# An adaLN attention and gMLP block on one core: the projection stage rearranged (transposes rounded by ScalarE from PSUM, four V tiles in step, w_qkv in column halves, modulation sums spread)

## The chip, the cores and the metric

The kernel runs on one core of one Trainium2 chip. A core has five engines that run side by side, each through its own queue in order: TensorE (PE, matrix multiplication; PEld is its weight load), VectorE (DVE), ScalarE (ACT), GpSimd (POOL) and SyncE (SP), which here only issues DMAs. They meet through semaphores. Data lie in SBUF (128 partitions), matmuls write into PSUM banks, and only PE, DVE and ACT are used on PSUM here. The metric is the device time of one execution in microseconds (us), the median of the runs.

## The reference

A block with S = 2048 tokens, D = 448 channels and 16 heads of 28 channels, in float32:

```
mod = (silu(c) @ w_mod).reshape(1, 6, 1, -1)
sa, ca, ga, sb, cb, gb = (mod[:, i] for i in range(6))
h = layernorm(x) * (1 + ca) + sa
q, k, v = split(h @ wqkv)                       # 16 heads of 28
x = x + ga * (softmax(q k^T / sqrt(28)) v @ wo)
h = layernorm(x) * (1 + cb) + sb
z = gelu(h @ w_in);  z1, z2 = halves(z);  z2 = layernorm(z2)
out = x + gb * ((z1 * (w_sp @ z2 + b_sp)) @ w_out)
```

The change touches the way to q, k and v: the modulation `mod`, the first layer norm, its transposition and the projection `h @ wqkv`.

## The kernel before

**Precision.** PE multiplies a rounded format (`F32R`). To keep float32 accuracy a matrix is stored as a rounded high part `hi` and the rest `lo` (`sub`, L69 to 71: the full value minus `hi`), and a product is made from hi·hi, hi·lo and lo·hi. D = 448 is 3 chunks of 128 and a last one of 64; the last chunk is put on partitions 0 to 63 and again on 64 to 127, so that one matmul handles two parts of it. `STEPS` lists the 11 resulting matmuls. So a V tile (128 tokens, 448 channels) and a QK unit (128 of the 896 rows of q and k, 512 tokens) are 11 matmuls each.

**The order is written by hand.** The program runs under a manual schedule: each engine executes its instructions in the order in which the Python text issues them. PSUM banks come from a ring of seven (`ring`) and one more bank (`ps_o`) that the attention stage uses for its outputs. SBUF buffers rotate within a pool by name or tag, and a DMA into one is issued only when the previous use of that buffer is over; as SP's queue is in order, a DMA behind it waits too.

**Stages.** Tokens are handled in four groups `g` of 512 (four tiles of 128). In order:

- Loads (L149 to 176): `x` of group 0, four slices `wm` of `w_mod` (one pair of the three pairs of modulation vectors), then the V columns of `wqkv` in four chunks. The q and k columns are read by `load_w("qk", i)`, 896 columns at a time, after group 0's transposes.
- Modulation: `mod_acc(pair, k)` (L194 to 201) is one of four steps of VectorE that add up a pair's vectors over slices of `w_mod` in `acc`. `mod_col` (L203 to 211) turns a vector into per-partition columns (`col_ca`, `col_sa`, and later `col_sb`, `col_cb`) with five one-column matmuls for each vector and an add by VectorE; `mod_bc` (L213 to 216) broadcasts one over all partitions. Pair 0 is needed at once; pairs 1 and 2 are needed only after the attention stage has begun (`ga` and the second layer norm).
- Layer norm: `ln_stats(g)` (L220 to 234) takes mean and variance on VectorE and the reciprocal root `rs` on GpSimd (L94, L95). `ln_norm(g)` (L235 on) writes `xn` on VectorE (L238) and has GpSimd copy its last 64 columns once more (L248).
- `ln_transpose` (L97 to 124): 16 transposes on PE (L104) fill four banks `tp`; each chunk is scaled and shifted from PSUM into `hfull` (ACT L111 or DVE L113), rounded to `hi` (L118 or L120), and `lo` is subtracted (L71). In group 0 ScalarE takes chunks 0 and 1 and VectorE chunks 2 and 3; in the other groups ScalarE takes all four, and GpSimd subtracts. In group 0 the columns are made between the transposes and these steps, and PE runs small matmuls on constants (`pe_fill`, L190) beside them.
- `v_tiles` (L251 to 258) and `qk_unit` (L260 to 273). A QK unit is copied out by ScalarE (`qf`), rounded by ScalarE (`qh`), its low part subtracted by GpSimd (`ql`), and both are stored to DRAM (`qk_scr`) by SP.
- The loop over `g` (L316 to 374). For each group: two V tiles, transposes of group g+1, statistics and normalisation of group g+2, two more V tiles, then QK units m = 0 and 3. Group 0 makes three V tiles ahead (two of them in step), then the hi and lo parts of the q and k weights (`weight_part`, L77 on, ScalarE for hi, VectorE and GpSimd in turn for lo), and a memset of V's spare columns (L362). Group 3 makes its QK units before its V tiles and begins to load head 0. `mod_acc` of pairs 1 and 2 stand at the end of groups 1 and 2; `mod_bc("ga")` and `mod_col(sb)` stand in group 2, the last pair's after the loop.
- A stretch of 20 QK units (m = 4, 1, 5, 2, 6 for four groups) in which each unit carries four score matmuls `mt` (`m_first`, `m_mm`, L385 to 393): scores of head 0 and part of head 1 for the row maximum, which VectorE reduces (L393). 80 `mt` in all.
- Then the attention loop over heads, the output projection and the gMLP, which the change leaves alone.

Of the kernel before, what the change touches and what calls it, by code (L numbers as in the profile page):

```python
# [20 lines left out]
NG = 4  # L21
# [12 lines left out]
def tile_adaln_mha_gmlp(ctx, tc, x, wqkv, wo, w_in, w_spT, b_sp, w_out, cT, w_mod, out):  # L34
# [35 lines left out]
    def sub(eng, dst, a, hi):  # L70
        eng.tensor_tensor(out=dst, in0=a, in1=hi.bitcast(F32), op=ALU.subtract)  # L71
# [2 lines left out]
        eng.dma_start(dst[0:64], src)  # L74
        eng.dma_start(dst[64:128], src)

    def weight_part(dst, i, raw, hi_eng, lo_eng, zero=True):  # L77

        n = raw.shape[-1]
        h = dst[:, i if i < 3 else 6, :n]  # L80
        if hi_eng is act:
            act.activation(h, raw, AF.Copy)
        else:
            hi_eng.tensor_copy(h, raw)
        if i < 3:
            sub(lo_eng, dst[:, 3 + i, :n], raw, h)
        else:
            sub(lo_eng, dst[0:64, 7, :n], raw[0:64], h[0:64])
            if zero:
                pool.memset(dst[64:128, 7, :n].bitcast(F32), 0.0)  # L90

    def rstd_of(var, rs, n):

# [54 lines left out]

    def load_mod(pair, eng):  # L149
        for k in range(4):  # L150
            wms[pair, k] = e1.tile([112, 2, D], F32, name="wm", bufs=4)
            eng.dma_start(wms[pair, k], w_mod[:, pair, k])

    def load_x(g, eng):
# [3 lines left out]
        for t in range(4):  # L158
            xts[4 * g + t] = xg[:, t, :]

    def load_w(kind, i, eng):
        c0, n = (2 * D, D) if kind == "v" else (0, 2 * D)
        raw = e1.tile([128, 2 * D], F32, name="raw", bufs=4)[:, :n]
        if i < 3:
            eng.dma_start(raw, wqkv[i * 128 : (i + 1) * 128, c0 : c0 + n])
        else:
            load_z(eng, raw, wqkv[384:448, c0 : c0 + n])
        raws[kind, i] = raw

    cc_t = e1.tile([112, 4], F32, name="cc_t", bufs=1)  # L170
    sp.dma_start(cc_t, cT)
# [1 line left out]
    load_mod(0, sp)  # L173
    for i in (0, 2, 1, 3):
        load_w("v", i, sp)
    pool.memset(wv[64:128, 7, :].bitcast(F32), 0.0)
    pool.memset(wqk[64:128, 7, :].bitcast(F32), 0.0)

# [6 lines left out]

    wu = ring.tile([128, 512], F32, name="wu", tag="s")

    def pe_fill(n):
        for _ in range(n):
            pe.matmul(wu[:, 0:128], ones, ones, start=True, stop=True)  # L190

    accs = {}

# [6 lines left out]
        else:  # L200
            dve.scalar_tensor_tensor(out=acc, in0=wm, scalar=silu[:, k : k + 1], in1=acc, op0=ALU.mult, op1=ALU.add)

    def mod_col(*parts):  # L203
        pc = ring.tile([128, 512], F32, name="pc", tag="s")
        for i, (nm, acc, plus1) in enumerate(parts):
            for c, r, e in ((0, 0, 128), (1, 0, 128), (2, 0, 128), (3, 0, 64), (3, 64, 128)):
                pe.matmul(
                    pc[r:e, 4 * i + c : 4 * i + c + 1], acc[:, c * 128 : c * 128 + e - r], ones[:112, 0:1], start=True, stop=True
                )
        for i, (nm, acc, plus1) in enumerate(parts):  # L210
            dve.tensor_scalar(out=cols[nm], in0=pc[:, 4 * i : 4 * i + 4], scalar1=plus1, scalar2=None, op0=ALU.add)

    def mod_bc(nm, acc):  # L213
        pc = ring.tile([128, 512], F32, name="pc", tag="s")
# [18 lines left out]
    def ln_norm(g):  # L233
        mv, rs = mv1.pop(g)
        res = []  # L235
        for t in range(4):
            xn = e1.tile([128, 512], F32, name="xn", bufs=4)
            dve.tensor_scalar(  # L238
                out=xn[:, :D],
                in0=xts.pop(4 * g + t),  # L240
                scalar1=mv[:, t, 0:1],
                scalar2=rs[:, t : t + 1],
                op0=ALU.subtract,
                op1=ALU.mult,
            )
            res.append(xn)
        for xn in res:
            pool.tensor_copy(xn[:, D:], xn[:, 384:D])  # L248
        return res

    def v_tiles(*kts):  # L251
        pvs = [ring.tile([128, 512], F32, name="pv", tag="s") for _ in kts]
        for j, (a, b) in enumerate(STEPS):
            for kt, pv in zip(kts, pvs):
                g, t = divmod(kt, 4)
                pe.matmul(pv[:, :D], hT[g][:, a, t * 128 : (t + 1) * 128], wv[:, b, :], start=j == 0, stop=j == NST - 1)  # L256
        for kt, pv in zip(kts, pvs):
            dve.tensor_copy(V[:, kt, :, 0:DH], pv[:, :D].rearrange("p (h d) -> p h d", d=DH))

    def qk_unit(m, g, mid=None):  # L260
        pq = ring.tile([128, 512], F32, name="pq", tag="s")
        for j, (a, b) in enumerate(STEPS):
            if mid and j in mid:
                mid[j]()
            pe.matmul(pq, wqk[:, b, m * 128 : (m + 1) * 128], hT[g][:, a, :], start=j == 0, stop=j == NST - 1)  # L265
        f = stage.tile([128, 512], F32, name="qf")
        act.activation(f, pq, AF.Copy)  # L267
        hi = stage.tile([128, 512], F32R, name="qh")
        act.activation(hi, f, AF.Copy)  # L269
        lo = stage2.tile([128, 512], F32R, name="ql")  # L270
        sub(pool, lo, f, hi)
        for i, t in enumerate((hi, lo)):
            sp.dma_start(qk_scr[i][m * 128 : (m + 1) * 128, g * 512 : (g + 1) * 512], t.bitcast(F32))

    ln_stats(0)
    mod_acc(0, 0)
    mod_acc(0, 1)
    xns = ln_norm(0)
    mod_acc(0, 2)
    mod_acc(0, 3)  # L280
    def wv_hi(i):
        act.activation(wv[:, i if i < 3 else 6, :], raws["v", i], AF.Copy)

    def wv_lo(i):
# [3 lines left out]
        else:  # L288
            sub(pool, wv[0:64, 7, :], raw[0:64], wv[0:64, 6, :])

    for i in (0, 2):
        wv_hi(i)
        wv_lo(i)

    def wv_rest(c):
        if c == 2:
            wv_hi(1)
            wv_lo(1)
        if c == 1:
            wv_hi(3)  # L300
            wv_lo(3)

    def mod_first():
        pe_fill(4)
        mod_col(("ca", accs[0][:, 1, :], 1.0), ("sa", accs[0][:, 0, :], 0.0))
        pe_fill(10)

    ln_transpose(
        xns, e1, hT[0], cols["ca"], cols["sa"], (act, act, dve, dve), (pool, pool, dve, dve), mod_first, wv_rest
    )  # L310
    load_x(1, sp)
    for i in range(4):
        load_w("qk", i, sp)
    ln_stats(1)
    xns = ln_norm(1)
    for g in range(NG):  # L316
        if g + 2 < NG:
            load_x(g + 2, sp)
        if g in (0, 2):
            load_mod(1 + g // 2, sp)  # L320
        if g == 3:
            early.close()
            stk = att.enter_context(tc.tile_pool(name="stk", bufs=1))
            kq = {}
            for i, (nm, pad) in enumerate((("k0", 64), ("q0", 0), ("q2", 16), ("k2", 0), ("q1", 8), ("k1", 8))):
                if pad:
                    stk.tile([128, pad], F32, name=f"pad{i}")
                kq[nm] = stk.tile([128, S], F32R, name=f"{nm[0]}st{nm[1]}")
            kst, qst = ([kq[f"{n}{i}"] for i in range(3)] for n in "kq")
            npool = att.enter_context(tc.tile_pool(name="npool", bufs=2))  # L330

            def load_head(h, c0=0, c1=S):
                k, q = kst[h % 3], qst[h % 3]
                if h < 2 and c0 == 0:
                    pool.memset(k[64:86, :].bitcast(F32), 1.0)
                for r0, i in ((0, 0), (56, 1), (28, 0)):
                    sp.dma_start(k[r0 : r0 + 28, c0:c1].bitcast(F32), qk_scr[i][D + h * DH : D + (h + 1) * DH, c0:c1])
                for r0, i in ((0, 0), (28, 1), (56, 0)):
                    sp.dma_start(q[r0 : r0 + 28, c0:c1].bitcast(F32), qk_scr[i][h * DH : (h + 1) * DH, c0:c1])

            load_head(0, 0, 1536)
            for m in (0, 3):
                qk_unit(m, g)
            load_head(0, 1536, S)
        if g == 0:
            v_tiles(0, 1)
            v_tiles(2)
        else:
            v_tiles(4 * g)
            v_tiles(4 * g + 1)  # L350
        if g == 0:
            for i in range(4):
                weight_part(wqk, i, raws.pop(("qk", i)), act, (dve, pool)[i % 2], False)
        if g + 1 < NG:
            ln_transpose(xns, e1, hT[g + 1], cols["ca"], cols["sa"], (act,) * 4)
        if g + 2 < NG:
            ln_stats(g + 2)
            xns = ln_norm(g + 2)
        if g > 0:
            v_tiles(4 * g + 2)  # L360
        else:
            pool.memset(V[:, :, :, DH:32], 1.0)  # L362
        v_tiles(4 * g + 3)
        if g == 2:
            mod_bc("ga", accs[1][:, 0, :])
            mod_col(("sb", accs[1][:, 1, :], 0.0))
        if g < 3:
            for m in (0, 3):
                qk_unit(m, g)
        if g in (1, 2):  # L370
            for k in range(4):
                mod_acc(g, k)
    mod_col(("cb", accs[2][:, 0, :], 1.0))
    mod_bc("gb", accs[2][:, 1, :])
    late_e.close()

# [165 lines left out]
                    for fn, a in when.pop(e):  # L542
                        fn(*a)

    for i, (m, g) in enumerate((m, g) for m in (4, 1, 5, 2, 6) for g in range(NG)):
        if i == 4:
            pool.memset(kst[2][64:86, :].bitcast(F32), 1.0)
        qk_unit(m, g, {j: m_first for j in (1, 4, 7, 10)})

    for u in range(NU + 1):  # L550
        for fn, a in events.pop(u, []):
# [390 lines left out]
```

## Time and profile before

| | us |
|---|---|
| median of the 3 runs | 1466.33 (1465.02 to 1467.49) |
| the profiled execution's own time | 1466.46 |
| its span in the profile | 1464.7 |
| first transpose on PE | 12.79 |
| first V matmul | 21.81 |
| first QK matmul | 34.54 |
| first `mt` | 96.71 |

A page of the profile gives the busy time of each engine over the span, the span in slices, and groups of equal instructions. Further views are cut from the same trace: the waits of an engine with what ended them, tables of busy time by stretch, and timelines, where each line is a run of alike instructions with its start and its length. L12 is a line of the program below. Busy time by stretch (us, span of core 0; PEclk is the granted clock of TensorE, 1.00 is full; the counts of instructions stand in brackets):

```profile
core 0: us, PE busy (x) PEld busy (x) DVE busy (x) ACT busy (x) POOL busy (x), PEclk, DMA share, GB/s
20.00:45.00 25.00, 21.38 (x112) 17.76 (x111) 20.14 (x34) 15.12 (x22) 20.88 (x20) 1.00 0.58 170
45.00:75.00 30.00, 27.00 (x137) 23.51 (x135) 16.99 (x27) 13.43 (x20) 21.92 (x22) 0.94 0.53 146
75.00:96.70 21.70, 21.70 (x110) 18.80 (x111) 7.54 (x12) 4.93 (x8) 8.86 (x6) 1.00 0.49 146
166.60:300.00 133.40, 133.37 (x728) 76.91 (x727) 112.87 (x190) 95.41 (x193) 5.20 (x6) 1.00 0.19 46
```

Here a reader compares PE's busy time with the length of a stretch: what is missing is PE waiting. In the last two lines nothing is missing.

### The profile page before, as it was taken

The numbers are of one execution on the slowest core, as the hardware profiler recorded it, in microseconds if no ns is written. First come the engines' busy times: TensorE is split into PE (matmuls) and PEld (weight loads), VectorE is DVE, ScalarE is ACT, GpSimd is POOL, SyncE is SP. The second block draws the span as 40 slices with busy tenths as digits, with TensorE's granted clock in tenths as the row PEclk, the third lists the DMA queues.
The fourth block names the chain that finished last, engine by engine and source line by source line (L and its number), as shares of the span: only waits on it lengthen the run. The fifth ranks groups of instructions, "written<-read, shape, count | busy, mean of one in ns | idle before, by whom it ended". The sixth has DMA issues, their size and how long they took to land.

```text
span 1464.7 us, 19637 instructions
## 1 busy us (share of the span) xinstructions
PE 1436.5 (98%) x7314; PEld 1015.3 (69%) x7314; DVE 884.6 (60%) x1440; ACT 733.1 (50%) x1390; POOL 302.0 (21%) x273
## 2 busy tenths in 40 slices
PE   5899999999999999999999999999999999999999
PEld 5787755555555555555555555888988888888887
DVE  6557888888888888888888832921552411413114
ACT  3523577677677767767776786442432211211111
POOL 6734200000002011001000021520763400302002
PEclk9999999999999999999999999999999999999999
DMA  7554401221022211221012004442002321313223
GB/s 220 146 163 151 145 9 46 52 49 43 15 52 53 53 39 40 53 51 41 21 47 52 11 19 139 151 149 101 8 14 99 119 77 67 113 64 106 84 69 107
DMA packets 56133, 111.24 MB, mean 76 GB/s; under 512 B 11901, under 2 KB 22781, under 8 KB 53517
## 3 DMA queue, kind: packets, MB, share of 16 engines
q1 hardware_dynamic: 55868, 109.76, 25.1%
q8 instruction: 57, 0.93, 0.3%
q10 hardware_dynamic: 168, 0.23, 0.1%
q14 instruction: 40, 0.32, 0.1%
HBM read 75.89 MB, written 29.48 MB: 72 GB/s over the span
## 4 chain that ended last, share of the span: by engine, by line
PE 92%; DVE 2%; POOL 2%; DMA 2%; issue 1%; ACT 0%; SPq 0%; ACTq 0%; DVEq 0%; POOLq 0%
PE st_ps L419 18%; PE mt L388 16%; PE o_ps L434 16%; PE acc L825 7%; PE acc L827 7%; PE acc L826 7%; PE z_ps L779 5%; PE z_ps L717 5%; PE pq L265 4%; PE y_ps L866 2%; PE y_ps L865 2%; PE y_ps L867 2%; PE pv L256 1%; PE tp L104 1%; POOL heapD L71 1%
## 5 line engine op out<-in xcount | busy, mean ns | idle before, releaser
L393 DVE TENSOR_REDUCE pm<-mt 128x1 f32<-128x512 f32 x1024 | 632.0, 681 | 121.8 <-PE mt L388 121.4
L423 ACT ACTIVATE P<-st_ps 128x512 f32<-128x512 f32 x1024 | 514.2, 618 | 154.3 <-PE st_ps L419 153.9
L419 PE MATMUL st_ps<-qst,kst 86*128 86x512 f32 x1024 | 409.8, 411 | 0.0
L388 PE MATMUL mt<-kst,qst 84*128 84x512 f32 x1024 | 406.6, 397 | 0.3 <-DVE pm L393 0.3
L419 PEld LDWEIGHTS st_ps<-qst,kst 86*128 86x128 f32 x1024 | 193.1, 189 | 144.8 <-issue 82.2
L434 PE MATMUL o_ps<-P,V 128*32 128x512 f32 x2048 | 247.5, 598 | 0.0
L388 PEld LDWEIGHTS mt<-kst,qst 84*128 84x128 f32 x1024 | 194.8, 190 | 38.3 <-DVE pm L393 0.7
L71 DVE TENSOR_TENSOR wsp_l<-raw_sp,wsp_h 128x512 fp32r<-128x512 f32 x64 | 53.7, 841 | 185.7 <-ACT wsp_h L762 185.7
L762 ACT ACTIVATE wsp_h<-raw_sp 128x512 fp32r<-128x512 f32 x64 | 40.3, 631 | 229.1 <-DMA raw_sp<-in_w_spT_dram 187.3
L434 PEld LDWEIGHTS o_ps<-P,V 128*32 128x32 f32 x2048 | 54.1, 109 | 123.5 <-issue 116.6
L71 POOL TENSOR_TENSOR heapD<-u,heapD 128x512 fp32r<-128x512 f32 x27 | 44.7, 1692 | 254.0 <-ACT heapD L844 170.2
L460 POOL TENSOR_TENSOR osb<-osb,rb 128x512 f32<-128x512 f32 x15 | 19.2, 1281 | 349.6 <-DMA rb<-r_scr 192.0
L265 PE MATMUL pq<-heapD 128*128 128x512 f32 x308 | 85.8, 396 | 2.9 <-DVE heapD L71 2.9
L825 PE MATMUL acc<-wsp_h,heapD 128*128 128x512 f32 x224 | 87.6, 391 | 0.6 <-DVE u L842 0.6
L827 PE MATMUL acc<-wsp_h,heapD 128*128 128x512 f32 x224 | 87.3, 390 | 0.0
L826 PE MATMUL acc<-wsp_l,heapD 128*128 128x512 f32 x224 | 87.2, 389 | 0.0
L265 PEld LDWEIGHTS pq<-heapD 128*128 128x128 f32 x308 | 58.0, 189 | 16.4 <-DVE heapD L71 3.4
L71 POOL TENSOR_TENSOR nl<-nf,nh 16x128 fp32r<-16x128 f32 x16 | 7.2, 453 | 285.5 <-issue 152.3
L267 ACT ACTIVATE qf<-pq 128x512 f32<-128x512 f32 x28 | 16.7, 597 | 70.1 <-PE pq L265 70.1
L870 DVE TENSOR_TENSOR x2t<-x2t,y_ps 128x448 f32<-128x448 f32 x12 | 7.5, 622 | 72.9 <-PE y_ps L867 72.9
L825 PEld LDWEIGHTS acc<-wsp_h,heapD 128*128 128x128 f32 x224 | 42.1, 188 | 9.7 <-DVE u L842 1.4
L71 POOL TENSOR_TENSOR ql<-qf,qh 128x512 fp32r<-128x512 f32 x28 | 36.4, 1304 | 59.7 <-ACT qh L269 47.2
(150 smaller groups left out, 1693.3 us busy)
## 6 DMA issues: line engine op xcount, KB each, us to landing
raw_sp<-in_w_spT_dram SPq DMA_DIRECT2D x64, 256.0 KB
kst<-qk_scr SPq DMA_DIRECT2D x45, 224.0 KB
qst<-qk_scr SPq DMA_DIRECT2D x45, 224.0 KB
qk_scr<-qh SPq DMA_DIRECT2D x28, 256.0 KB
qk_scr<-ql SPq DMA_DIRECT2D x28, 256.0 KB
z_scr<-z1t SPq DMA_DIRECT2D x28, 256.0 KB
z<-z_scr SPq DMA_DIRECT2D x28, 256.0 KB
wm<-in_w_mod_dram SPq DMA_DIRECT2D x12, 392.0 KB
```

The lines of the kernel that those rows point to most:

```text
L71: eng.tensor_tensor(out=dst, in0=a, in1=hi.bitcast(F32), op=ALU.subtract)
L265: pe.matmul(pq, wqk[:, b, m * 128 : (m + 1) * 128], hT[g][:, a, :], start=j == 0, stop=j == NST - 1)
L388: pe.matmul(mt, qst[h % 3][0:84, t * 128 : (t + 1) * 128], kst[h % 3][0:84, kb * 512 : (kb + 1) * 512], start=True, stop=True)
L393: dve.tensor_reduce(out=pms[h][:, t, kb : kb + 1], in_=mt, axis=AX.X, op=ALU.max)
L419: pe.matmul(st, kst[h % 3][0:86, kt * 128 : (kt + 1) * 128], qst[h % 3][0:86, qb * 512 : (qb + 1) * 512], start=True, stop=True)
L423: act.activation(p, st, AF.Exp, scale=SCALE)
L434: pe.matmul(otile[h][32 * qb : 32 * qb + 32, :], V[:, kt, h, :], ptiles.pop((u, qb)), start=kt == 0, stop=kt == NT - 1)
L717: pe.matmul(ps_t, w1[:, b, f * 128 : (f + 1) * 128], h2T[g][:, a, :], start=j == 0, stop=j == NST - 1)
L779: pe.matmul(ps_t[:, :D], h2T[g][:, a, tt * 128 : (tt + 1) * 128], w2[:, b, hf * D : (hf + 1) * D], start=j == 0, stop=j == NST - 1)
L825: pe.matmul(acc[f], z2[st][:, 0, fs], hi, start=st == 0, stop=False)
L826: pe.matmul(acc[f], z2[st][:, 0, fs], lo, start=False, stop=False)
L827: pe.matmul(acc[f], z2[st][:, 1, fs], hi, start=False, stop=st == NT - 1)
```

## The change

It touches the part up to the stretch with `mt`, and the number of `mt` in a unit of that stretch.

- *Start.* `pe_fill(8, xts[3])` runs as soon as `x` is there; the fills around the columns are 4 and 3 instead of 4 and 10. `xn`'s last 64 columns are copied by ScalarE in group 0, and written by a second instruction of VectorE in the other groups.
- *Columns of group 0.* `mod_col` makes the columns of chunks 0 and 2 first and those of 1 and 3 afterwards, each with its own bank and its own adds.
- *Transposes of group 0.* VectorE makes all four `hfull` from PSUM, ScalarE writes the rounded `hi` from PSUM directly with the same scale and shift; `lo` is subtracted by GpSimd for chunk 0 and by VectorE for 2, 1 and 3.
- *V tiles 0 to 3* run in step: each of the 11 steps for all four tiles before the next step; the fourth tile uses the bank of `ps_o`, and the steps come in another order.
- *w_qkv* for q and k is read as part `a` (columns 0 to 511, into the buffers of `wm`) and part `b` (512 to 895, into `raw`). `hi` is by ScalarE and `lo` by VectorE; `a` is made before the first QK units, `b` in group 1 (chunk 0 after V tile 4, the rest after V tile 7).
- *QK units* m = 0 and 3 of group 0 run in step; transposes of group 1 follow; units m = 1 and 2 of group 0 then run at once and no longer in the stretch with `mt`, which has 18 units, the first 8 with five `mt` and the others with four.
- *Modulation pairs 1 and 2*: their sums stand one behind V tiles 6 and 7 and one behind each QK unit of group 1, the same in group 2 for pair 2; `mod_bc("ga")` and `mod_col(sb)` move from group 2 to the end of group 1. `wm` of pair 2 takes the `raw` buffers.
- *Loads*: `x` of group 1 is issued ahead of the q and k columns, group 2's behind part `b`, group 3's at the start of group 1.

```diff
-    def mod_col(*parts):
+    def mod_col(parts, cs=(0, 1, 2, 3)):
...
     ln_stats(0)
+    pe_fill(8, xts[3])
     mod_acc(0, 0)
...
+    parts = ("ca", accs[0][:, 1, :], 1.0), ("sa", accs[0][:, 0, :], 0.0)
+    c02, c13 = (mod_col(parts, cs) for cs in ((0, 2), (1, 3)))
+    pe_fill(3)
...
+    def h_full(c):
...
+        dve.tensor_scalar(
+            out=fs[c], in0=tps[c], scalar1=cols["ca"][:, c : c + 1], scalar2=cols["sa"][:, c : c + 1], op0=ALU.mult, op1=ALU.add
+        )
+
+    def h_hi(c):
+        act.activation(
+            hT[0][:, c if c < 3 else 6, :], tps[c], AF.Identity, scale=cols["ca"][:, c : c + 1], bias=cols["sa"][:, c : c + 1]
+        )
...
+    c02()
+    h_full(0)
+    h_hi(0)
+    h_full(2)
+    h_hi(2)
+    c13()
...
+    pvs = v_mm((0, 1, 2), [STEPS[j] for j in (0, 1, 2, 6, 3, 4, 7, 5, 8, 9, 10)], 3)
+    qk_part("a", 0)
+    qk_part("a", 2)
     ln_stats(1)
+    qk_part("a", 1)
+    qk_part("a", 3)
+    load_mod(1, sp)
+    for a in pvs[:3]:
+        v_copy(*a)
     xns = ln_norm(1)
+    v_copy(*pvs[3])
+    qk_unit((0, 3), 0)
+    ln_transpose(xns, e1, hT[1], cols["ca"], cols["sa"], (act,) * 4)
+    qk_unit((1,), 0)
+    qk_unit((2,), 0)
+    pool.memset(V[:, :, :, DH:32], 1.0)
+    ln_stats(2)
+    xns = ln_norm(2)
+    for g in range(1, NG):
+        if g == 1:
+            load_x(3, sp)
...
+        v_tile(4 * g)
+        if g == 1:
+            qk_part("b", 0)
+        v_tile(4 * g + 1)
         if g + 1 < NG:
             ln_transpose(xns, e1, hT[g + 1], cols["ca"], cols["sa"], (act,) * 4)
         if g + 2 < NG:
             ln_stats(g + 2)
             xns = ln_norm(g + 2)
...
+        for k in range(2):
+            v_tile(4 * g + 2 + k)
+            if g < 3:
+                mod_acc(g, k)
+        if g == 1:
+            for i in (2, 1, 3):
+                qk_part("b", i)
+            load_mod(2, sp)
         if g < 3:
...
+            for k, m in enumerate((0, 3)):
+                qk_unit((m,), g)
+                mod_acc(g, 2 + k)
+            if g == 1:
+                mod_bc("ga", accs[1][:, 0, :])
+                mod_col((("sb", accs[1][:, 1, :], 0.0),))()
...
-    for i, (m, g) in enumerate((m, g) for m in (4, 1, 5, 2, 6) for g in range(NG)):
+    units = [(m, g) for m in (4, 1, 5, 2, 6) for g in range(NG) if g > 0 or m not in (1, 2)]
+    for i, (m, g) in enumerate(units):
...
-        qk_unit(m, g, {j: m_first for j in (1, 4, 7, 10)})
+        qk_unit((m,), g, {j: m_first for j in ((1, 3, 5, 7, 9) if i < 8 else (1, 4, 7, 10))})
```

## The prediction

> **What bounds the kernel now.** I read the page's busy shares first, then PE's waits over the first 300 us, then tables of stretches, then each engine's timeline up to 97 us, where the change ends.
>
> ```profile
> PE 1436.5 (98%) x7314; PEld 1015.3 (69%) x7314; DVE 884.6 (60%) x1440; ACT 733.1 (50%) x1390; POOL 302.0 (21%) x273
> ...
> PE tp L104 <- DVE xn L238: 12.8, 1, 12.8
> PE pv L256 <- DVE V L258: 3.0, 1, 3.0
> PE pq L265 <- DVE heapD L71: 2.9, 1, 2.9
> PE pv L256 <- DVE st L225: 0.5, 1, 0.5
> ```
>
> PE is the bound: 1464.7 − 1436.5 = 28.2 us idle in all, 12.8 of it before its first transpose. So only two kinds of gain exist: PE starting real work sooner, and the 3.0, 2.9 and 0.5 us waits. The stretch from 96.71 (first `mt`) is full of matmuls:
>
> ```profile
> 67.90:71.30 3.40, 1.18 (x6) 1.11 (x7) 3.23 (x4) 1.49 (x3) 3.32 (x3) 1.00 1.04 271
> 71.30:74.80 3.50, 3.50 (x9) 2.48 (x8) 0.62 (x1) 0.00 (x0) 0.74 (x1) 0.51 0.38 104
> 96.70:166.60 69.90, 69.58 (x299) 56.09 (x298) 55.02 (x81) 23.83 (x40) 26.72 (x21) 1.00 0.48 163
> ```
>
> Columns: stretch, length, busy PE, PEld, DVE, ACT, POOL with counts, granted clock, DMA share, GB/s. The third line is the 20 QK units with four `mt` each, 69.9/20 = 3.50 us a unit. The first two show a 3 us PE wait followed by 3.4 us at half clock, which costs about 1.7 us of matmul work.
>
> ```profile
> 12.80 3.58 POOL L248 COPY xn<-xn 128x64 f32<-128x64 f32 x4 [1.34 <-DVE xn L238]
> 19.94 0.81 DVE L113 TENSOR_SCALAR hfull<-tp,col_ca,col_sa 128x512 f32<-128x512 f32 x1
> 20.00 0.78 ACT L111 ACTIVATE hfull<-tp,col_sa,col_ca 128x512 f32<-128x512 f32 x1 [3.64 <-DVE col_sa L211]
> 21.81 3.90 PE L256 MATMUL pv<-wv,heapD 128*128 128x448 f32 x16
> 46.76 2.53 POOL L71 TENSOR_TENSOR ql<-qf,qh 128x512 fp32r<-128x512 f32 x2
> 58.36 1.04 POOL L95 TENSOR_TENSOR rs<-rs,mhalf 128x4 f32<-128x4 f32 x1 [0.17 <-POOL rs L94]
> 59.44 1.78 DVE L238 TENSOR_SCALAR xn<-xg,mv,rs 128x448 f32<-128x448 f32 x4 [1.63 <-POOL rs L95]
> 63.29 6.24 DVE L201 SCALAR_TENSOR_TENSOR acc<-wm,silu,acc 112x896 f32<-112x896 f32 x3
> 65.19 6.85 POOL L71 TENSOR_TENSOR heapD<-hfull,heapD 128x512 fp32r<-128x512 f32 x4 [0.79 <-ACT heapD L118]
> 70.12 3.46 PE L256 MATMUL pv<-wv,heapD 128*128 128x448 f32 x11 [3.00 <-DVE V L258]
> 75.68 10.27 PE L265 MATMUL pq<-heapD 128*128 128x512 f32 x44
> ```
>
> Columns: start, length, engine, line, operation, output and inputs, count, idle before it and what ended it. The reader should see two engines feeding PE late: GpSimd (POOL) with its subtractions and the reciprocal root `rs`, and VectorE behind `rs` with `xn` and the modulation sums `acc`. VectorE's three sums ran from 63.29 to 69.53, 2.08 each, while GpSimd worked; the same operation took 1.15 alone at 11.16.
>
> **The change, part by part.** I follow the new order with these durations and write the time at which each step ends.
>
> *Front.* GpSimd's copies (3.58 us, which held the transposes until 16.97) go to ScalarE. PE now gets 8 fills from 8.14 us, when x is there, so the transposes may run warm: 16 at 0.109 instead of 0.213. The sums end at 16.28 as before; four column matmuls (20 took 1.91, so 0.4) behind the remaining fills and the two small adds (0.16) give 17.64. `h_full(0)` on VectorE from PSUM, 0.81: 18.45. ScalarE's rounded `h_hi(0)` reads the same PSUM tile and waits for VectorE: 0.78 more and a start, 19.3, against 21.81: 2.5 us sooner. If PE is still at half clock through transposes, fills and columns it is 20.7, 1.4 later; I take the middle, +0.7.
>
> The Trainium skill ("TensorE: Matmul & The Clock Gate", Part 4) holds that transposes do not count as work for the clock. The rows disagree: behind 16 transposes alone (4.18 us from 12.79, 0.26 each) eight fills of the same shape took 1.06, 0.13 each. By the page the front would be the late one, 0.7 us worse than my middle.
>
> *V tiles 0–3 in step.* 44 matmuls, same number as before, spaced 0.204 (a tile of 11 is 2.24): 28.3. The fourth tile has the idle output bank. Its lows (`h_lo`, `wv_lo`) come later in the new step order; VectorE needs 0.69 for each and is through with them near 24, under these matmuls; uncovered, one costs 0.7.
>
> *Column halves of w_qkv.* 896-wide lows took 6.02 for two beside GpSimd (32.24) and caused the 2.9 us wait. A half of 512 is 0.69 alone, four are 2.8 and lie with the statistics (2.6) under the V tiles, to about 29.5; two QK units in step use them up to 33.45 (22 matmuls at 0.234, 5.15). So the 2.9 and 0.5 us waits go. Bound: from nothing to 1.5 (the 64-partition low beside GpSimd).
>
> *QK m=1, 2 of group 0 pulled forward.* Transposes of group 1, 1.7, then 22 matmuls: 40.35. They leave the later stretch, where a unit without its `mt` is 2.57 (10.27/4): 5.1 us come off there. V4 waits 0.7 for a GpSimd low; V5 ends at 45.6.
>
> *What they queue on GpSimd.* From 34.75 (after two ScalarE copies of 0.60 and 0.63): two `ql` 2.55, four lows of group 1 5.56 (1.39 each), two more `ql` 2.52, the V memset 0.95, `rs` 1.36 = 12.9, so `rs(2)` ends at 47.7; `xn(2)` follows at 0.53 each (0.42 plus a second instruction for 64 columns, my estimate 0.1, replacing GpSimd's copies; bounds 0 to 0.2, 0.4 us a group). PE, done at 45.6, has its transposes only at 48.3 to 51.5: the first new stall, about 4 us net. It lies ahead of the next one, so it costs nothing of its own.
>
> *Sums spread.* GpSimd: four lows of group 2 to 57.25, `rs(3)` 58.65; VectorE's `xn(3)` to 60.85. In VectorE's queue then: V6 copy 0.53, sum 0.69, V7 copy 0.53, sum 2.0 (beside `ql`), three lows of half b 1.5 to 1.7, two sums 2.35 = 7.9, so 68.8. PE does V6, V7 (4.5) and two QK units (5.1) from 51.5 to 61.1 and reaches `mod_bc(ga)`, moved up one group; it needs the last sum. **Stall: 61.1 to 68.8, 7.7 us**, where before PE could run on with V8 to V10. GpSimd's queue isn't held by it. SP's is: the loads of the third pair wait for half b's lows and hold two stores of q and k behind them, but those are read only past 90, which covers them.
>
> *From 68.8 to the first `mt`*: mod_bc and column 1.4 (94.75 to 96.13 in the old timeline), V8–15 8 × 2.24 = 17.9, transposes of group 3 1.7, four QK units 10.1, the last pair's columns 1.4 = 32.5: 101.3. Half clock after the stall: 1.7 by the old row (bounds 0.8 to 2.5, since after a wait this long the resume is surely cold and may lie anywhere in a window of 3.4). Front 0.7. Sum 103.7, against 96.71: +7.0. Minus the two units: −5.1. **Net +1.9 us.**
>
> The Trainium skill (same page, Part 1) says that a PE idle for a window of about 3.4 us falls to half rate and needs about as long to return. The 71.30 row agrees after 3.0 us of waiting. It speaks against the change: by the page the one long stall is charged in full, up to 1.7; were it wrong, the sum would be +0.2.
>
> *Later.* 18 units instead of 20, the first 8 with five `mt`: 8×5 + 10×4 = 80, the same. VectorE's reduction is 681 ns, and five take 3.4 of the unit's 3.7 (11×0.234 + 5×0.234), so it is hidden; uncovered, 40 × 0.05 = 2 at most. I take 0.
>
> The profiled execution is 1466.46, its span 1464.7; the median of the runs is 1466.33, 0.13 lower. 1466.46 + 1.9 = **1468.4**. About 0.2%, 2.9 us, is what can be told from no change.
>
> **Rivals.**
> 1. *VectorE arrives in time (faster).* Its chain hangs on GpSimd's `rs(3)`; were the last sum done by 61.1, first `mt` is 61.1 + 32.5 = 93.6 with no half clock: −3.1 − 5.1 = −8.2, 1458.3. It decides faster from a stall under about 2.5 us. For it: GpSimd's subtractions may run at 1.28 rather than 1.39, and sums at 1.15 rather than 2.05. Against: that is at most 1.5 + 1 us of the 7.7 (then 1466). Chance 0.16, 0.13 of it below 1463.5.
> 2. *Lost turns (slower).* VectorE and GpSimd take turns: the pair of rows 63.29 and 65.19 shows each sum a GpSimd instruction late, and in the 32.24 row two lows took 6.02. Five two-input instructions of VectorE stand in the 7.9 us; I counted one lost turn. Two or three more, 1.3 each, give 1471.0 to 1472.3; the first already passes 0.2%. Chance 0.20, 0.02 of it unchanged. "GPSIMD Engine Reference" (section 1, Specifications) of the Trainium skill states that shared SBUF interface, for VectorE instructions with two SBUF inputs; the rows agree.
> 3. *The front does not move.* ScalarE and VectorE are serialised on each transposed tile, and if PE is cold or the column pairs are late, V starts at 21 to 21.8; GpSimd's queue shifts with it and the net is +3 to +4, 1469.4 to 1470.5. Against: the two engines' instructions are fewer than before. Chance 0.12 (0.05 same, 0.07 slower).
>
> **How the numbers follow.** The forecast has 0.52; its own range (half clock −0.9/+0.8, front ±0.7, one turn ±1.3, as roots of squares ±1.7) is 1466.7 to 1470.1, two thirds below 1469.4: 0.33 same, 0.19 slower. Faster 0.13; same 0.33 + 0.03 + 0.02 + 0.05 = 0.43; slower 0.19 + 0.18 + 0.07 = 0.44. The range 1463 to 1472.3 leaves out most of rival 1 and rival 2's far end.
>
> **What would show it.** The first `pv` near 19.3; no wait for VectorE's low at the first QK unit; PE's transposes of group 2 waiting for `xn` near 48; one PE wait of 6 to 9 us at `mod_bc`, ended by VectorE's sum, with a half-clock stretch behind it; the first `mt` at 102 to 105; the rest shorter by 5. The forecast is wrong if that wait is under 3 us, if PE waits twice as long elsewhere, or if the `mt` units exceed 3.8 us.

## The result: slower, by more than the range

The changed kernel took 1472.93 us, the median of 4 runs (1472.63 to 1473.11), the kernel before 1465.67 us beside it (4 runs, 1464.90 to 1467.49). The ratio is 1.0048, with a 95% interval of 1.0035 to 1.0062: 7 us slower. The forecast was 1468.4 and the range ended at 1472.3. The direction of the sum was right, its size was not.

The busy shares on the page of the changed kernel (busy us, share of the span, instructions), and then its longest waits of PE over the first 300 us (line and tile, what was waited for: us in total, times, longest):

```profile
PE 1442.8 (98%) x7316; PEld 1023.6 (70%) x7316; DVE 883.0 (60%) x1461; ACT 733.6 (50%) x1398; POOL 288.4 (20%) x254
```

```profile
PE wu L197 <- DMA xg<-in_x_dram: 8.7, 1, 8.7
PE pc L236 <- DVE acc L208: 7.1, 1, 7.1
PE tp L104 <- DVE xn L261: 3.1, 4, 2.5
PE pv L276 <- POOL heapD L71: 0.7, 1, 0.7
```

The old waits at `pq` (2.9) and at the V tile (3.0) are gone. In their place stand 7.1 us at `mod_bc` (L236 here) and 3.1 us at the transposes of group 2. But the first line shows something that the waits do not: PE is *busy* 6.3 us longer than before (1436.5), 5.5 of it behind the first V matmul, where the matmuls are the same as before. That is time at a lower clock. PE's timeline of the changed kernel (start, length, then the operation as before; the trace counts each matmul of the fills, of `mod_bc` and of `mod_col` twice, so `x10` at L217 is the five one-column matmuls of one vector):

```profile
19.64 10.75 PE L276 MATMUL pv<-wv,heapD 128*128 128x448 f32 x44 [0.21 <-ACT heapD L346]
30.23 5.20 PE L291 MATMUL pq<-heapD 128*128 128x512 f32 x22
...
50.05 0.33 PE L104 MATMUL tp<-ident,xn 128*128 128x128 f32 x1 [2.47 <-DVE xn L261]
...
54.67 5.85 PE L276 MATMUL pv<-wv,heapD 128*128 128x448 f32 x22
60.36 5.15 PE L291 MATMUL pq<-heapD 128*128 128x512 f32 x22
72.62 1.83 PE L236 MATMUL pc<-acc,ones 112*128 112x448 f32 x2 [7.11 <-DVE acc L208]
74.24 1.59 PE L217 MATMUL pc<-ones,acc 112*128 112x1 f32 x10
75.76 7.12 PE L276 MATMUL pv<-wv,heapD 128*128 128x448 f32 x22
```

Twenty-two V matmuls take 4.65 us at full clock (at 58.48 in the kernel before); here they take 5.85 and 7.12. The table of stretches of the same kernel, cut where the granted clock changes (columns as in the prediction, the clock third from the end):

```profile
16.16:19.57 3.41, 3.27 (x32) 3.01 (x31) 2.20 (x7) 1.71 (x4) 2.22 (x2) 1.00 1.01 356
19.57:22.99 3.42, 3.35 (x9) 3.02 (x10) 3.39 (x4) 3.42 (x8) 3.32 (x3) 0.50 0.95 274
46.88:50.30 3.42, 0.95 (x5) 0.45 (x3) 0.82 (x3) 0.00 (x0) 2.48 (x4) 1.00 1.09 295
50.30:53.71 3.41, 2.75 (x11) 2.09 (x11) 3.41 (x10) 1.12 (x2) 0.00 (x0) 0.50 0.55 205
53.71:57.12 3.41, 3.41 (x14) 3.15 (x13) 2.37 (x8) 3.00 (x6) 2.60 (x3) 0.50 0.43 118
67.36:70.78 3.42, 0.00 (x0) 0.00 (x0) 3.42 (x5) 0.00 (x0) 2.46 (x1) 1.00 0.43 119
70.78:74.19 3.41, 1.57 (x2) 0.84 (x3) 1.66 (x2) 0.00 (x0) 0.00 (x0) 0.50 1.00 318
74.19:77.60 3.41, 3.41 (x16) 3.15 (x15) 0.79 (x2) 0.00 (x0) 0.00 (x0) 0.50 0.78 225
77.60:81.02 3.42, 3.42 (x11) 3.03 (x10) 0.62 (x1) 0.00 (x0) 0.00 (x0) 0.50 0.00 0
...
110.00:174.60 64.60, 64.60 (x280) 52.45 (x279) 55.14 (x82) 21.39 (x36) 24.11 (x19) 1.00 0.48 160
```

Up to the stretch with `mt` the clock is halved for six windows of 3.41 us, 20.5 us in all, against one window in the kernel before. (The record of the clock begins with its rise to full, at 12.75 here and at 16.73 in the kernel before; for the time ahead of it the tables print 1.00 and say nothing.) The last line is the stretch with `mt`: full of matmuls, with 18 units.

The account against the profile before: first `mt` at 109.88 instead of 96.71, +13.2; the stretch from there to the first matmul of the attention loop 64.7 instead of 70.4, −5.7; all that follows −0.8. Together +6.6, the difference of the spans (1471.3 and 1464.7).

### The profile page after: what moved, and what is told of

Same layout as the page of the kernel before. It is cut to its first block, busy times and chain, and to the rows that moved or that the text cites. A ratio compares the mean times of both kernels' runs of the same rounds, so it can differ in the third digit from the quotient of the medians.

```text
span 1471.3 us, 19655 instructions
## 1 busy us (share of the span) xinstructions
PE 1442.8 (98%) x7316; PEld 1023.6 (70%) x7316; DVE 883.0 (60%) x1461; ACT 733.6 (50%) x1398; POOL 288.4 (20%) x254
## 4 chain that ended last, share of the span: by engine, by line
PE 91%; DVE 3%; DMA 2%; POOL 2%; issue 1%; ACT 1%; SPq 0%; ACTq 0%; DVEq 0%; POOLq 0%
PE st_ps L492 18%; PE mt L461 16%; PE o_ps L507 16%; PE acc L899 6%; PE acc L901 6%; PE acc L900 6%; PE z_ps L853 5%; PE z_ps L791 5%; PE pq L291 4%; PE pv L276 2%; PE y_ps L940 2%; PE y_ps L941 2%; PE y_ps L939 2%; DMA raw_sp<-in_w_spT_dram 1%; PE tp L104 1%
## 5 line engine op out<-in xcount | busy, mean ns | idle before, releaser
L291 PEld LDWEIGHTS pq<-heapD 128*128 128x128 f32 x308 | 58.2, 190 | 12.9 <-issue 0.2
```

## The experiments

Ten kernels were run in three batches, each batch with runs of the kernel before on the same chip. Those medians of before lie between 1465.43 and 1467.07, so ratios are compared and not times alone. The theory at the start was that the long wait at `mod_bc` and the half clock behind it make the loss.

**mod_bc moved back.**

```diff
-            if g == 1:
-                mod_bc("ga", accs[1][:, 0, :])
-                mod_col((("sb", accs[1][:, 1, :], 0.0),))()
...
             ln_transpose(xns, e1, hT[g + 1], cols["ca"], cols["sa"], (act,) * 4)
+        if g == 2:
+            mod_bc("ga", accs[1][:, 0, :])
+            mod_col((("sb", accs[1][:, 1, :], 0.0),))()
```

> The changed kernel with mod_bc(ga) and its column moved back from the end of group 1 to group 2, behind the transposes of group 3. Theory A (the one long wait at mod_bc and the half clock behind it are the loss): PE goes on with V8, V9 and the transposes while VectorE sums, the 7.1 us wait falls under 1.5 us, no half clock near 71 to 81 (4.2 us), first mt at 99 to 102 instead of 109.9, time 1462 to 1465. Rival B (VectorE's queue itself is late, so the wait only goes to the next V copy): first mt stays above 106, time 1469 or more.

Measured: 1464.54 us (11 runs), ratio to before 0.9992 (0.9983 to 1.0001). First `mt` at 99.94. PE's waits of this run (its lines are one higher than in the changed kernel):

```profile
PE tp L105 <- DVE xn L262: 3.4, 4, 2.5
...
PE pc L237 <- ACT hfull L112: 0.9, 1, 0.9
```

The wait at `mod_bc` fell from 7.1 to 0.9 us, no half clock follows it, and nothing took its place. Theory A holds; B falls. One edit of place takes the loss away: 1.0048 to 0.9992, some 8 us.

**Layer norm of group 2 ahead of the two pulled QK units.**

```diff
+    ln_stats(2)
+    xns = ln_norm(2)
     qk_unit((1,), 0)
     qk_unit((2,), 0)
     pool.memset(V[:, :, :, DH:32], 1.0)
-    ln_stats(2)
-    xns = ln_norm(2)
```

> The changed kernel with statistics and normalisation of group 2 put ahead of the two QK units pulled forward, so that on GpSimd rs(2) comes before their two subtractions and the memset. Theory A: rs(2) ends near 46 instead of 49.45, PE's wait for xn of group 2 falls from 3.1 to about 2, the half clock of 50.3 to 57.1 goes or halves, and the wait at mod_bc stays (6 to 8 us, with a half clock behind it), since VectorE's chain moves by less: time 1469.5 to 1471.5. Rival B (the first wait is only cover for the second, and nothing ahead of mod_bc matters): 1472.5 to 1473.5.

Measured: 1472.48 us (5 runs, 1470.35 to 1474.99), ratio 1.0048 (1.0035 to 1.0062), the same as the changed kernel's. The waits for `xn` came to 2.6 us, and the wait at `mod_bc` was 7.4. The time is rival B's. The profile stands between the two: the half clock at the transposes was one window instead of two, `mod_bc` came at 71.33 instead of 72.62, and the first `mt` at 108.18 instead of 109.88. With the runs 4.6 us apart, a gain of 1 to 2 us is neither shown nor ruled out.

**Both edits.**

> Both edits together. Theory A: the two waits are of two causes and their half clocks go with them: first mt at 98 to 100, time 1460.5 to 1463, below the kernel before. Rival B: PE, no longer held at mod_bc, waits for GpSimd's lows of groups 2 and 3 instead: 1465 to 1469.

Measured: 1463.17 us (11 runs), ratio 0.9983 (0.9974 to 0.9992), first `mt` at 97.97. With `mod_bc` out of the way the earlier layer norm may gain a little, 0.9992 to 0.9983, but the two intervals overlap. The time is 0.2 above what theory A gave.

**Fills in the waits.** Constant matmuls keep PE at work while it waits; nothing else moves (each group of fills takes one bank of the ring).

```diff
+        if g == 1:
+            pe_wait(9)
         if g + 1 < NG:
             ln_transpose(
...
             if g == 1:
+                pe_wait(27)
                 mod_bc("ga", accs[1][:, 0, :])
```

> The changed kernel with idle PE work put into its two long waits and nothing else moved: 9 constant matmuls ahead of the transposes of group 2 (some 2.4 us) and 27 ahead of mod_bc (some 7.1 us). Theory C (half clock after the waits is a cost of its own, about 2.5 us at the first and 4.2 us at the second): no half clock between 50 and 81, first mt 103 to 105.5, time 1466.5 to 1469. Rival D (the waits alone cost, the half clock lies beside work that waits anyway): 1472 to 1473.5.

Measured: 1471.63 us (5 runs, 1469.67 to 1475.50), ratio 1.0045 (1.0032 to 1.0059), first `mt` at 106.40. It fits neither theory. PE's timeline of this run says why:

```profile
61.26 6.19 PE L203 MATMUL wu<-ones 128*128 128x128 f32 x54
69.95 1.83 PE L242 MATMUL pc<-acc,ones 112*128 112x448 f32 x2 [2.50 <-DVE acc L214]
71.58 1.58 PE L223 MATMUL pc<-ones,acc 112*128 112x1 f32 x10
```

The fills were too few: they ended 2.5 us before the sum was there, and the clock was halved from 69.71 to 76.53 after all. At the first wait they did their work: there the clock stayed full. So the run did not test the second wait, and it was made again with more.

**More fills.** The same with `pe_wait(38)` ahead of `mod_bc`.

> The fills of the run before, with 38 instead of 27 constant matmuls ahead of mod_bc, so that PE is never idle there (27 left 2.5 us, behind which the clock was halved for 6.8 us). Theory C (the half clock is a cost by itself): no half clock between 50 and 81, first mt 103 to 105.5 against 106.4 with 27 fills and 109.9 without, time 1467.5 to 1470. Rival D (half clock lies beside waits and costs nothing): first mt stays within 0.5 us of 106.4, 1471 to 1473.

Measured: 1468.81 us (11 runs), ratio 1.0021 (1.0010 to 1.0031). The table of stretches of this run:

```profile
60.00:70.00 10.00, 10.00 (x73) 9.30 (x72) 7.92 (x15) 2.88 (x6) 4.45 (x5) 1.00 0.00 1
70.00:80.00 10.00, 9.96 (x68) 9.00 (x67) 4.61 (x7) 0.27 (x1) 0.00 (x0) 1.00 0.80 228
```

Full clock throughout. `mod_bc` still comes at 72.76, so the sum is as late as in the changed kernel; only the half clock behind the two waits is gone, and with it 4 us (1.0048 to 1.0021). Theory C holds by the time and the clock. The first `mt`, at 106.21, missed its bounds, because this execution lost more at the start, where its clock was halved from 14.51 to 17.92 and from 21.34 to 24.75: its first QK matmul stands at 31.35, against 28.57 in the run before and 30.23 in the changed kernel. Counted from there, the first `mt` comes 74.9 us later, against 77.8 with too few fills and 79.7 without.

The price of the place of `mod_bc` can be parted further. It comes at nearly the same time in three of the executions: at 72.62 in the changed kernel, at 72.76 in this run and at 72.74 in the one with `mod_bc` moved back. From there to the first `mt` it is 37.3, 33.4 and 27.2 us. So of the 10.1 us between the first and the last, 3.8 are half clock and 6.3 are V tiles and transposes that PE could have done during the wait.

**The two pulled QK units put back.**

```diff
-    qk_unit((1,), 0)
-    qk_unit((2,), 0)
...
-    units = [(m, g) for m in (4, 1, 5, 2, 6) for g in range(NG) if g > 0 or m not in (1, 2)]
+    units = [(m, g) for m in (4, 1, 5, 2, 6) for g in range(NG)]
```

> The changed kernel without the pull of QK units m=1, 2 of group 0: they go back into the stretch of 20 units with four mt each. Theory A (the pull only fills PE's wait for GpSimd, and adds two subtractions to GpSimd's queue): first mt at 106 to 108, 2 to 4 us sooner, since GpSimd has 2.5 us less to do; the stretch with mt 5.7 us longer; the wait at mod_bc stays 6 to 9 us; time 1474.5 to 1477. Rival E (the two subtractions on GpSimd are what made the change lose): 1469 or less.

Measured: 1477.64 us (6 runs), ratio 1.0074 (1.0061 to 1.0087). First `mt` at 108.46, only 1.4 us sooner and not the 2 to 4 expected; the stretch behind it took 70.44. The pull is a gain of some 4 us within the changed kernel, a little more than theory A gave it; E falls. Its two matmul groups run where PE would wait for the lows of group 1: here PE waited 2.7 us there for ScalarE's rounding and 0.8 for GpSimd.

**mod_bc moved forward in the kernel before.** The same place, without the rest of the change.

```diff
-        if g == 2:
-            mod_bc("ga", accs[1][:, 0, :])
-            mod_col(("sb", accs[1][:, 1, :], 0.0))
...
             for k in range(4):
                 mod_acc(g, k)
+            if g == 1:
+                mod_bc("ga", accs[1][:, 0, :])
+                mod_col(("sb", accs[1][:, 1, :], 0.0))
```

> The kernel before with one thing of the change: mod_bc(ga) and its column stand at the end of group 1, behind the pair's sums, instead of in group 2. Theory A (the place of mod_bc is enough to lose by): PE waits there 8 to 11 us for VectorE's sums, a half clock of two or three windows follows, the old 3.0 us wait goes, first mt at 100 to 104 instead of 96.7, time 1469 to 1473. Rival F (it costs only with the change's longer VectorE chain): wait under 4 us, 1465 to 1468.

Measured: 1475.03 us (5 runs), ratio 1.0057 (1.0045 to 1.0069). First `mt` at 105.17. Both lie above theory A's bounds, by 2 us and by 1. PE's wait and the four windows of half clock of this run:

```profile
PE pc L215 <- DVE acc L201: 9.4, 1, 9.4
```

```profile
61.68:65.09 3.41, 0.00 (x0) 0.00 (x0) 3.37 (x5) 0.00 (x0) 3.41 (x5) 0.50 0.19 70
65.09:68.51 3.42, 0.00 (x0) 0.00 (x0) 3.35 (x3) 0.00 (x0) 0.13 (x1) 0.50 1.02 221
68.51:71.92 3.41, 3.23 (x13) 2.41 (x13) 0.66 (x2) 0.00 (x0) 0.00 (x0) 0.50 1.03 266
71.92:75.33 3.41, 3.41 (x9) 3.06 (x10) 0.16 (x1) 0.00 (x0) 0.00 (x0) 0.50 0.60 144
```

That one move costs the old kernel as much as it costs the new one. F falls. The place of `mod_bc` is the cause, shown from both sides.

**Only the one-column matmuls moved behind V8 and V9.**

```diff
             if g == 1:
                 mod_bc("ga", accs[1][:, 0, :])
-                mod_col((("sb", accs[1][:, 1, :], 0.0),))()
...
         v_tile(4 * g + 1)
+        if g == 2:
+            mod_col((("sb", accs[1][:, 1, :], 0.0),))()
```

> The changed kernel with mod_bc left at the end of group 1 and only the one-column matmuls of sb moved behind V8 and V9. In the changed kernel's profile the half clock lasted from 70.78 to 81.02 though PE worked again from 72.62, the one-column matmuls from 74.24 to 75.8 among it. Theory H (a window with the one-column matmuls in it does not bring the clock back): after the wait the half clock is one window (3.4 us) shorter, two windows or fewer from the resume, first mt 1 to 1.8 us sooner, time 1471 to 1472. Rival I (the length is where the windows fall and nothing else): three windows as before, 1472.5 to 1473.5.

Measured: 1472.02 us (8 runs, 1470.19 to 1474.62), ratio 1.0036 (1.0020 to 1.0051). The interval holds the changed kernel's ratio too, so the time decides nothing. The clock does. The first `mt` came at 107.15, and its windows happened to fall as in the run with the earlier layer norm, so the two can be laid side by side. That run, with the columns right behind `mod_bc`:

```profile
68.62:72.03 3.41, 0.70 (x1) 0.50 (x2) 2.53 (x3) 0.00 (x0) 0.00 (x0) 0.50 0.88 233
72.03:75.45 3.42, 3.42 (x15) 2.71 (x14) 0.79 (x2) 0.00 (x0) 0.00 (x0) 0.50 1.03 317
75.45:78.86 3.41, 3.41 (x11) 3.02 (x10) 0.00 (x0) 0.00 (x0) 0.00 (x0) 0.50 0.39 112
```

And this run, with V8 right behind `mod_bc`:

```profile
68.77:72.18 3.41, 0.05 (x1) 0.08 (x1) 3.18 (x5) 0.00 (x0) 0.00 (x0) 0.50 0.68 182
72.18:75.60 3.42, 3.42 (x7) 2.42 (x8) 0.62 (x1) 0.00 (x0) 0.00 (x0) 0.50 1.03 303
75.60:79.01 3.41, 3.41 (x18) 3.14 (x17) 0.62 (x1) 0.00 (x0) 0.00 (x0) 1.00 0.61 178
```

In both the second window is full by PE's busy time. With the one-column matmuls in it the clock stayed halved for one more window; with `mod_bc` and V matmuls alone it came back. H holds for these two executions; what all the profiles say of it stands in the last section.

**Layer norms drawn ahead.** On top of `mod_bc` moved back (the load and the layer norm of group 2 are taken out at their old places):

```diff
+    load_x(3, sp)
+    ln_stats(2)
     qk_unit((0, 3), 0)
     ln_transpose(xns, e1, hT[1], cols["ca"], cols["sa"], (act,) * 4)
+    xns = ln_norm(2)
     qk_unit((1,), 0)
...
+        if g + 2 < NG:
+            ln_stats(g + 2)
         if g + 1 < NG:
             ln_transpose(xns, e1, hT[g + 1], cols["ca"], cols["sa"], (act,) * 4)
         if g + 2 < NG:
-            ln_stats(g + 2)
             xns = ln_norm(g + 2)
```

> The changed kernel with mod_bc back in group 2 and the layer norms drawn ahead on GpSimd: x of group 3 is loaded ahead of the first QK stores, statistics of group 2 stand before the first QK units (rs(2) ahead of all four ql), statistics of group 3 before the transposes of group 2 (rs(3) ahead of their four lows). Theory A (what is left of the loss is rs behind subtractions in GpSimd's queue): no PE wait for xn, short waits for GpSimd's lows near V4 (2 to 3 us in pieces), no half clock at 50, first mt at 94 to 97, time 1457.5 to 1461. Rival G (GpSimd's queue is full anyway, and what rs gains the lows lose): first mt above 98, 1462 or more.

Measured: 1462.82 us (10 runs), ratio 0.9972 (0.9963 to 0.9981), first `mt` at 97.63. A miss for theory A: there is no wait for `xn`, but PE waited 3.6 us for GpSimd's lows at V4 and V5, and the clock was halved from 47.03 to 50.44. Rival G's time fits, its first `mt` (above 98) does not. VectorE's timeline of this run has the reason, eight instructions that took 2.68 in the changed kernel:

```profile
38.69 8.56 DVE L261 TENSOR_SCALAR xn<-xg,mv,rs 128x448 f32<-128x448 f32 x8 [1.47 <-POOL rs L95]
```

And GpSimd's, beside it:

```profile
38.63 2.69 POOL L71 TENSOR_TENSOR ql<-qf,qh 128x512 fp32r<-128x512 f32 x2
41.28 2.69 POOL L71 TENSOR_TENSOR heapD<-hfull,heapD 128x512 fp32r<-128x512 f32 x2
44.13 3.07 POOL L71 TENSOR_TENSOR heapD<-hfull,heapD 128x512 fp32r<-128x512 f32 x2 [0.16 <-ACT heapD L118]
```

The normalisation now runs beside the subtractions, and the two engines take turns: six of VectorE's eight instructions took 1.26 to 1.53 us and ended 0.05 to 0.25 us behind the end of a subtraction; the other two, which began as one subtraction ended and before the next, took 0.50.

**The first two `ql` by VectorE, `mod_bc` behind V10.** On top of the run with the layer norms drawn ahead:

```diff
-    qk_unit((0, 3), 0)
+    qk_unit((0, 3), 0, eng=dve)
...
             v_tile(4 * g + 2 + k)
+            if g == 2 and k == 0:
+                mod_bc("ga", accs[1][:, 0, :])
+                mod_col((("sb", accs[1][:, 1, :], 0.0),))()
```

> The run with the early layer norms, and two more edits: the low parts ql of the first two QK units are subtracted by VectorE (idle there) instead of GpSimd, so that GpSimd reaches the lows of group 1 about 2.5 us sooner, and mod_bc with its column stands behind V10. Theory A (GpSimd's queue of lows is what PE waits for at V4 and V5): the four waits there (3.6 us) fall to 1 to 2, no half clock at 47, no wait at mod_bc, first mt at 92 to 95 instead of 97.6, time 1457.5 to 1460.5. Rival G (the lows of group 1 wait for ScalarE, which copies and rounds them, or for turns with VectorE): waits stay above 3 us, 1461.5 or more.

Measured: 1459.64 us (6 runs), ratio 0.9953 (0.9936 to 0.9971). Below both kernels: 0.5% below the one before. PE's waits of this run:

```profile
PE pv L276 <- POOL heapD L71: 1.1, 1, 1.1
PE pc L236 <- DVE V L280: 0.9, 1, 0.9
```

Theory A holds for what PE waited for at V4 and V5. The first `mt`, at 95.59, is 0.6 above its bounds, and a wait of 0.9 stayed at `mod_bc`, where the expectation had none. Behind it the clock was halved for one window, with `mod_bc`, its one-column matmuls (0.94 us) and the wait in the window before:

```profile
67.67:71.08 3.41, 2.50 (x16) 1.72 (x15) 3.20 (x7) 2.71 (x4) 3.18 (x2) 1.00 1.01 316
71.08:74.50 3.42, 3.42 (x11) 3.05 (x11) 0.59 (x1) 0.00 (x1) 1.60 (x1) 0.50 0.54 161
```

So about 1.7 us, half of the second window, are still lost there. What each of the two edits gives alone was not tried.

## Why the prediction was wrong

**What held.** The mechanism was the forecast's: the front and the old waits gain, and the stall at `mod_bc` takes it back and more. GpSimd's queue was put at 12.9 us from the first `ql` to `rs(2)`. It took 12.88:

```profile
36.57 2.54 POOL L71 TENSOR_TENSOR ql<-qf,qh 128x512 fp32r<-128x512 f32 x2 [5.89 <-ACT qh L296]
...
48.41 1.04 POOL L95 TENSOR_TENSOR rs<-rs,mhalf 128x4 f32<-128x4 f32 x1
...
60.40 1.04 POOL L95 TENSOR_TENSOR rs<-rs,mhalf 128x4 f32<-128x4 f32 x1
```

The stall was put at 7.7 us and was 7.1; its length fits better than its place, since PE came 3.7 us later than forecast (with the 0.7 of front) and the last sum 3.0. VectorE's chain from `xn(3)` to the last sum was put at 7.9 (its items add up to 7.6 to 7.8) and took 8.3 (64.15 to 72.47). The units that left the stretch with `mt` were put at −5.1 and gave −5.7.

**The step that failed: the price of half clock.** The prediction said: "Half clock after the stall: 1.7 by the old row (bounds 0.8 to 2.5...)". That price was one window with PE busy in all of it. The profile shows three windows behind the stall, with PE busy for 8.4 us of them, so some 4.2 lost by that count. The run with 38 fills measures it: at full clock it took 33.4 us from `mod_bc` to the first `mt`, the changed kernel 37.3. So the half clock cost 3.8 us and not 1.7, and 0.95 was missing in the 32.5 us that the prediction gave to the stretch without it. The bounds assumed that the clock comes back within 3.4 us of the resume. It took 8.4: PE resumed in the middle of one window, and the next, full by PE's busy time, held the one-column matmuls and was followed by another at half clock.

**The same price left out at the first stall.** The prediction said: "It lies ahead of the next one, so it costs nothing of its own." The wait of 2.47 us halved the clock too, from 50.30 to 57.12. Transposes and V tiles ran slow, so the transposed tiles reached ScalarE and GpSimd late. `rs(3)` ended at 61.4 instead of 59.4 (the prediction with its 0.7 of front); 1.1 of that was there at the first `ql` already. From `rs(2)` to `rs(3)` it took 12.0 us instead of 10.95. In the two runs with fills, where the clock was full there, it took 11.5. So some 0.5 us is half clock, and 0.5 was short in the prediction at any clock. A delay that ends in a wait of PE costs nothing; a delay that passes through PE into the queue of the engine that PE will wait for does.

**Smaller terms.** The front: `pv` began at 19.64, within its bounds, but the V tiles in step took 10.75 and not 9.0, with half clock from 19.57 to 22.99 (9.24 at full clock in the run with the columns behind V8 and V9), so the first QK matmul came at 30.2 and not at 29.0, and GpSimd's first `ql` 1.1 us late. In the ten executions profiled with this front the first V matmul lies anywhere between 19.0 and 22.0: at 19.0 to 20.0 in the five where the clock rose to full by 13.1 us and stayed there until 19 at least, at 21.2 to 22.0 in the four where it rose between 17.4 and 19.5, at 20.7 in one that rose at 11.1 and was halved again from 14.5 to 17.9. The prediction took the middle of a warm and a cold start; that this execution was one of the warm ones is luck. Its 0.4 us for four column matmuls read the 20 records of the old row as 20 matmuls; they are ten, so four take 0.76. The second instruction of `xn` takes 0.25 and not 0.1 (2.68 for a group instead of 2.12), above the bound given: 0.5 us a group. VectorE's chain lost two turns and not one (the first sum took 1.57, three lows 2.55; 1.16 and 1.48 in the run with 27 fills), but the second sum, put at 2.0, took 1.14: 0.4 in all.

The sum of it: 3.0 us more up to `mod_bc` (1.1 at the front, 1.0 from `rs(2)` to `rs(3)`, 0.5 for `xn`, 0.4 in VectorE's chain), 3.1 more from there to the first `mt` (37.3 instead of 32.5 + 1.7), and 1.4 less behind it (0.6 in the stretch, 0.8 later, which was not traced to a cause). That is 4.7, which is what lies between +1.9 and +6.6.

**The rivals.** Rival 1 did not happen. Rival 2 had nearly the right time, but by luck: it asked for two or three lost turns more than the one counted, and one more was lost, worth 0.4 us in the sum. Rival 3 was half right: the front's gain of 2.2 us at the first `pv` is partly given back behind it.

**The page's rule.** The prediction set the rule on the clock ("TensorE: Matmul & The Clock Gate", Part 1, in the Trainium skill) beside one window's price. The rule says that the window runs freely and that the clock falls after one idle window and returns after a busy one. The grid of 3.41 us agrees with every profile here. A wait of 2.47 us, with PE busy 0.95 in its window, was already enough to fall (a window with 1.55 us of QK matmuls, 63.95 to 67.36, was not), and a window in which PE was busy throughout was not always enough to return.

## What to carry to other kernels

An instruction that waits in PE's queue should stand as late as the use of its result allows, not as early as its inputs may be there: moving `mod_bc` up by one group cost 8 us in both kernels. Price a wait of a few microseconds as the wait and every window of half clock behind it, and count in which window the resume falls and what runs in it. When a queue of another engine sets the end, ask what its own inputs are late for: a slow clock on PE comes back through ScalarE and GpSimd.

## What the runs showed of the hardware that was not expected

*The clock behaved as if matmuls of one column were idle time.* The twelve profiled executions have 34 windows at half clock up to 112 us, and PE's busy time without these matmuls sorts them. All 21 windows with 3.1 us or more of other work were followed by full clock, all 13 with 2.8 us or less by another window at half clock. With the one-column matmuls counted in, five of these 13 were busy for 3.17 to 3.41 us: one each in the changed kernel, in the runs with the earlier layer norm, with 27 fills and with the two units put back, and in the old kernel with `mod_bc` moved. In the run with 27 fills PE resumed right at the start of the window, at 69.95, and 1.54 us of the first line are such matmuls:

```profile
69.71:73.12 3.41, 3.17 (x13) 2.35 (x13) 0.72 (x2) 0.00 (x0) 0.00 (x0) 0.50 0.98 305
73.12:76.53 3.41, 3.41 (x11) 3.06 (x10) 0.16 (x1) 0.00 (x0) 0.00 (x0) 0.50 0.65 199
```

They help the clock to fall, too. Eleven windows at the front began at full clock and hold 1.7 to 1.9 us of these matmuls. The five with 1.52 to 1.62 us of other work (3.20 to 3.30 busy in all, the window 16.16 to 19.57 of the changed kernel among them) were followed by half clock, the six with 1.73 or 1.74 us (3.41 in all) were not. It is not the missing tenth or two of a microsecond: windows of V and QK matmuls alone kept the clock with anything from 1.55 to 2.8 us of work, and lost it with 1.34 and less. Where the line lies for other matmuls is not settled here: windows of transposes with few or no fills lost the clock with 1.74 us (50.20 to 53.62 in the run with `mod_bc` moved back) and with 2.18 us (11.10 to 14.51 in the run with 38 fills), and kept it with 2.28 (11.68 to 15.09 in the run with 27).

*VectorE's normalisation, with one tensor input, takes turns with GpSimd's subtractions.* Eight instructions took 2.68 us alone and 8.56 beside them.
